# Long-run loads, one pool of accumulator banks, 2.25 frequency blocks and an inverse DFT by parity in a Nyströmformer and Hyena kernel

## The chip, the cores and the metric

The kernel runs on one core of a Trainium2 chip. The metric is device time in microseconds (us) of one execution; most executions of one kernel agree within 0.3 to 1%. A run is "slow" when it is over 1.5% above the fastest of the same kernel; ratios use fast runs alone. Besides the time, each run has one profiled execution, whose span (first to last instruction) is a few us shorter than the time.

Engines: PE is TensorE (matrix products), DVE is VectorE, ACT is ScalarE, POOL is GpSimd, which also issues the loads. Products write to an accumulator memory (PSUM), whose eight banks this kernel shares out among its buffer pools; an eviction is a DVE or ACT copy out of it.

## The reference, cut to what matters

```python
# q, k, v: [8 batches, 8 heads, 576 rows, 64]; m = 32 landmarks, scale = 1/8
q_lm = q.reshape(B, H, m, 18, D).mean(axis=3);  k_lm likewise
A  = softmax(scale * q    @ k_lm^T)          # 576 x 32 per head
Bm = softmax(scale * q_lm @ k_lm^T)          # 32 x 32
C  = softmax(scale * q_lm @ k^T)             # 32 x 576
Z  = Bm^T / (norm1 * norminf + 1e-6);  6 times: Z = 2 Z - Z Bm Z     # Newton
x  = (A @ Z @ C @ v)                         # heads side by side: [8, 576, 512]
x1, x2, x3 = split(x @ w_proj)               # 3 x 512 columns
x2c = irfft(rfft(x2, over rows) * rfft(filter, over rows))
out = (x1 * x2c * x3) @ w_out                # [8, 576, 512]
```

The kernel calls the first part of a batch its attention and the second its gate. It keeps the factors `ZC` (Z C v) and `A` apart, so that the projection works on `G = ZC @ w_proj` and the forward DFT on A. A real DFT of 576 rows has 289 frequencies; they are split by parity, so that only 288 rows are transformed.

## The kernel before

The parts that the change and the argument touch (cuts marked with `# ...`):

```python
ps_w: 2 buffers of 2 banks (big products)      # 4 banks
ps_t: 2 buffers of 1 bank, ps_s: 2 of 1 bank   # 2 + 2 banks

def load(b):                                   # k and q in runs of 64 floats = 256 bytes
    for c in range(NC): nc.gpsimd.dma_start(kn[:, c], kv[c])      # 6 transfers
    for c in range(NC): nc.gpsimd.dma_start(qn[:, c], qv[c // 3, c % 3])
    # ... v in 2 transfers, runs of 1,536 bytes

def attention(b):
    # ... landmark sums of head pairs (ps_s); 48 transposes into ps_t; Bm, its scaled inverse start (ps_s)
    for cc in range(3):
        RZ = newton(RZ, False)                 # ps_s, evicted by ACT and DVE
        pc = ps_t.tile(...)                    # scores of C, ps_t
        # ... 8 products, then exp on ACT
    # ... the same for A; C v into a ps_w buffer
    nc.vector.tensor_reduce(rA, eA, ...)       # row sums of A's softmax
    # ... A, AE (even and odd rows), AT (transposed A)

def gate(b, ZC, AE, AT):
    # ... G parts 1, 0, 2 and the forward DFT of A
    for f in range(3):                         # 3 frequency blocks of 96 rows
        # ... 4 products of 512 columns; X = copy (ACT); T = X * HH; Y = T0 + T1 (DVE)
    for j in range(4):
        # ... x1 (ACT) and gt = x1 * x3 (DVE), 8 products
        pi = wtile()                           # inverse DFT over 576 columns
        for f in range(3):
            for t in range(2):
                for e in range(2): matmul(pi[:, e, 0:288], Y[:, f, t, 128 j...], INV[:, f, t, 288 e...])
        nc.vector.tensor_tensor(y[:, j], pi, gt, op=mult)
    # ... out = y @ w_out in 5 row blocks (ps_t), copy, store

att = {0: attention(0)}; tables_fwd(); tables_inv(); filter_spectrum()
for b in range(8):
    load(b + 2); att[b + 1] = attention(b + 1); gate(b, *att.pop(b))
```

The order on each engine is made by a scheduler when the program is built; it mixes attention b+1 with gate b. Each engine then runs its own queue in that order.

The softmax here doesn't subtract the row's maximum and nothing guards it: scores larger than these inputs give would overflow.

## Time and profile before

The three runs before had a median of 358.37 us.

| what | value | view |
|---|---|---|
| span | 352.5 us | page |
| gate 0 starts / ends | 64.7 / 94.3 us | timeline, first G product and last output product |
| from the end of a gate to the end of the next | 38.0 us | timeline |
| PE busy in such an interval | 33.2 us | windows |
| gate 7 and the last stores | 323.5 to 352.5 us | timeline |

"Interval" below always means the third row: from the end of one gate's last output product to that of the next. The page of the kernel before; the first lines give busy us with the share of the span, the rows of digits the busy tenths in 40 slices, `q0` the queue of the loads:

```profile
span 352.5 us, 6549 instructions
...
PE 285.1 (81%) x2640; PEld 184.3 (52%) x2640; DVE 217.5 (62%) x464; ACT 159.5 (45%) x263; POOL 94.3 (27%) x150
...
PE   0586867699889899879888888979987988698793
...
PEclk9999999999999999999999999999999999999999
...
q0 software_dynamic: 82928, 16.85, 56.1%
```

The windows of two intervals (start and end, length; busy us with the number of instructions by engine; granted PE clock; DMA share; GB/s). The second has no load issues on POOL, and is as long:

```profile
209.29:247.33 38.04, 33.22 (x330) 21.53 (x330) 24.70 (x51) 18.40 (x31) 10.48 (x14) 1.00 0.72 79
...
247.00:285.00 38.00, 33.18 (x329) 21.53 (x327) 24.45 (x51) 18.38 (x31) 0.00 (x0) 1.00 0.11 32
```

PE is busy for 87% of an interval and far ahead of DVE and ACT. The timeline of PE: start, length, line, tiles, count, and the idle time before it with its cause. At the head of an interval, transposes (`pt`) and Newton pairs (`s<-RZ`) take turns, with waits on single evictions; later come waits of about a us on G and gt:

```profile
209.22 0.43 PE L161 MATMUL pt<-ident,kn 96*128 96x96 bf16 x6
209.49 0.30 PE L220 MATMUL s<-RZ 128*128 128x160 f16 x2
210.20 0.42 PE L161 MATMUL pt<-ident,kn 96*128 96x96 bf16 x6 [0.41 <-DVE kT L166]
...
220.38 0.90 PE L446 MATMUL w<-F,AE 96*128 96x288 f16 x6 [1.10 <-ACT G L439]
...
229.60 0.65 PE L476 MATMUL w<-AT,G 128*128 128x288 f16 x4 [0.78 <-ACT X L461]
...
232.66 0.65 PE L476 MATMUL w<-AT,G 128*128 128x288 f16 x4 [1.14 <-DVE gt L483]
```

The records of products overlap (a product of the inverse has a record of 287 ns, and the next one starts 132 ns after it). Charging each product only the time until the next one starts, or its own end where it comes earlier, a Newton product costs 130 ns in the kernel before (12 in an interval, 1.56 us).

### The profile page before, as it was taken

The numbers are of one execution on the slowest core, as the hardware profiler recorded it, in microseconds if no ns is written. First come the engines' busy times: TensorE is split into PE (matmuls) and PEld (weight loads), VectorE is DVE, ScalarE is ACT, GpSimd is POOL, SyncE is SP. The second block draws the span as 40 slices with busy tenths as digits, with TensorE's granted clock in tenths as the row PEclk, the third lists the DMA queues.
The fourth block names the chain that finished last, engine by engine and source line by source line (L and its number), as shares of the span: only waits on it lengthen the run. The fifth ranks groups of instructions, "written<-read, shape, count | busy, mean of one in ns | idle before, by whom it ended". The sixth has DMA issues, their size and how long they took to land.

```text
span 352.5 us, 6549 instructions
## 1 busy us (share of the span) xinstructions
PE 285.1 (81%) x2640; PEld 184.3 (52%) x2640; DVE 217.5 (62%) x464; ACT 159.5 (45%) x263; POOL 94.3 (27%) x150
## 2 busy tenths in 40 slices
PE   0586867699889899879888888979987988698793
PEld 0374743366465557546564646645754655364361
DVE  0148698987547854796456754785468656751651
ACT  1042263764366226542466237622654156625512
POOL 9934967700091006500280009200000000000000
PEclk9999999999999999999999999999999999999999
DMA  5999999930499019900694049901300050004104
GB/s 35 132 205 171 169 101 123 124 58 0 111 124 105 2 46 145 138 10 0 145 127 68 2 116 112 111 0 39 100 0 2 0 137 0 2 0 113 25 0 134
DMA packets 88718, 26.70 MB, mean 76 GB/s; under 512 B 76720, under 2 KB 83376, under 8 KB 88688
## 3 DMA queue, kind: packets, MB, share of 16 engines
q0 software_dynamic: 82928, 16.85, 56.1%
q1 hardware_dynamic: 5760, 9.44, 9.8%
q8 instruction: 20, 0.33, 0.4%
q14 instruction: 10, 0.08, 0.1%
HBM read 33.69 MB, written 9.44 MB: 122 GB/s over the span
## 4 chain that ended last, share of the span: by engine, by line
PE 50%; DVE 24%; ACT 10%; DMA 7%; POOL 4%; issue 3%; SPq 0%; DVEq 0%; ACTq 0%; POOLq 0%
PE w L488 9%; PE po L500 8%; DVE T L463 8%; PE w L476 6%; PE pt L161 4%; PE w L434 4%; DMA kn<-in_k_dram 4%; DVE y L492 4%; PE w L446 4%; PE w L265 3%; DVE gt L483 3%; ACT G L439 3%; ACT X L461 2%; PE pa L254 2%; PE pc L238 2%
## 5 line engine op out<-in xcount | busy, mean ns | idle before, releaser
L111 POOL DMA_DIRECT2D kn<-in_k_dram x48 | 37.2, 787 | 113.1 <-PE pt L161 111.7
L488 PE MATMUL w<-INV,Y 96*128 96x288 f16 x384 | 54.8, 287 | 0.2
L476 PE MATMUL w<-AT,G 128*128 128x288 f16 x256 | 41.7, 284 | 15.8 <-DVE gt L483 8.7
L500 PE MATMUL po<-wout,y 128*128 128x512 bf16 (+1 forms) x160 | 42.1, 380 | 5.3 <-ACT os L506 3.2
L463 DVE TENSOR_TENSOR T<-X,HH 96x2048 bf16<-96x2048 bf16 x24 | 28.7, 1217 | 24.0 <-ACT X L461 24.0
L488 PEld LDWEIGHTS <-Y 96*128 96x128 bf16 x384 | 35.1, 98 | 14.7 <-DVE Y L465 5.9
L476 PEld LDWEIGHTS <-G 128*128 128x128 bf16 x256 | 24.6, 96 | 32.5 <-issue 25.2
L113 POOL DMA_DIRECT2D qn<-in_q_dram x48 | 37.2, 783 | 9.7 <-DMA wproj<-in_moe_w_proj_dram 7.1
L506 ACT COPY os<-po 128x512 f32<-128x512 f32 (+1 forms) x32 | 18.7, 584 | 33.0 <-PE po L500 32.3
L492 DVE TENSOR_TENSOR y<-w,gt 128x576 bf16<-128x576 f32 x32 | 24.2, 757 | 15.0 <-PE w L488 15.0
L439 ACT CAST G<-w 128x1024 bf16<-128x1024 f32 x24 | 23.5, 1014 | 14.4 <-PE w L434 14.4
L166 DVE COPY kT<-pt 128x576 bf16<-128x576 bf16 x24 | 10.9, 457 | 26.2 <-PE pt L161 25.7
L500 PEld LDWEIGHTS <-y 128*128 128x128 bf16 (+1 forms) x160 | 14.7, 100 | 22.2 <-issue 8.6
L461 ACT CAST X<-w 96x1024 bf16<-96x1024 f32 x24 | 23.5, 1008 | 4.5 <-DVE T L463 3.2
L457 PE MATMUL w<-G,Ah 128*96 128x512 bf16 x96 | 23.8, 377 | 2.1 <-ACT G L439 1.4
L294 DVE TENSOR_REDUCE rA<-eA 96x48 f32<-96x1536 bf16 x8 | 14.0, 1748 | 15.0 <-ACT eA L258 15.0
L225 ACT CAST RZ<-s 128x256 f16<-128x256 f32 x40 | 14.9, 372 | 15.8 <-PE s L220 11.0
L446 PE MATMUL w<-F,AE 96*128 96x288 f16 x96 | 14.5, 285 | 8.4 <-ACT G L439 7.7
L226 DVE TENSOR_TENSOR RZ<-RZ,s 128x64 f16<-128x64 f16 x48 | 10.5, 218 | 14.5 <-ACT RZ L225 10.6
L434 PE MATMUL w<-wproj,ZC 128*64 128x512 bf16 x96 | 18.2, 390 | 0.5 <-ACT Ah L449 0.5
L220 PE MATMUL s<-RZ 128*128 128x160 f16 (+1 forms) x96 | 14.6, 235 | 4.9 <-DVE RZ L226 2.4
L161 PE MATMUL pt<-ident,kn 96*128 96x96 bf16 x192 | 15.3, 221 | 3.5 <-DVE kT L166 2.6
(205 smaller groups left out, 480.3 us busy)
## 6 DMA issues: line engine op xcount, KB each, us to landing
kn<-in_k_dram POOLq DMA_DIRECT2D x48, 96.0 KB, 4.3
qn<-in_q_dram POOLq DMA_DIRECT2D x48, 96.0 KB, 4.1
out_dram<-os SPq DMA_DIRECT2D x24, 192.0 KB, 2.5
out_dram<-os SPq DMA_DIRECT2D x24, 128.0 KB, 2.3
vb_103<-in_v_dram POOLq DMA_DIRECT2D x8, 288.0 KB, 6.3
vb_105<-in_v_dram POOLq DMA_DIRECT2D x8, 288.0 KB, 6.7
wproj<-in_moe_w_proj_dram POOLq DMA_DIRECT2D x1, 1536.0 KB, 13.7
out_dram<-os SPq DMA_DIRECT2D x24, 64.0 KB, 2.0
```

The lines of the kernel that those rows point to most:

```text
L111: nc.gpsimd.dma_start(kn[:, c], kv[c])
L113: nc.gpsimd.dma_start(qn[:, c], qv[c // 3, c % 3])
L161: nc.tensor.matmul(pt[:, c * R:(c + 1) * R], src[:, c, 2 * x:2 * x + 2, :].rearrange("p h d -> p (h d)"), ident[:R, :R], is_transpose=True ...
L434: nc.tensor.matmul(pg[64 * pp:64 * pp + 64, g, :], ZC[:, 2 * g + pp, :, :].rearrange("p h l -> p (h l)"), wproj[:, 2 * g + pp, Dm * jb:Dm ...
L439: nc.scalar.copy(G[:, :, Dm * jb:Dm * (jb + 1)], pg)
L446: nc.tensor.matmul(pf[:, par, 0:HS], AE[:, par, c, 128 * g:128 * g + 128], F[:, c, :, lo:lo + Q], start=(c == 0), stop=(c == 2))
L461: nc.scalar.copy(X, px[:R])
L463: nc.vector.tensor_tensor(T, X.unsqueeze(2).to_broadcast([R, 2, 2, Dm]), HH[:, f], op=ALU.mult)
L476: nc.tensor.matmul(px[:, e, 0:HS], G[:, g, lo:lo + P], AT[:, g, HS * e:HS * e + HS], start=(g == 0), stop=(g == 1))
L488: nc.tensor.matmul(pi[:, e, 0:HS], Y[:, f, t, P * j:P * j + P], INV[:, f, t, HS * e:HS * e + HS], start=(f == 0 and t == 0), stop=(f == NF ...
L492: nc.vector.tensor_tensor(y[:, j, :].rearrange("p (e s) -> p e s", e=2), pi[:, :, 0:HS], gt, op=ALU.mult)
L500: nc.tensor.matmul(po[:n], y[:, j, i0:i0 + n], wout[:, j, :], start=(j == 0), stop=(j == 3))
```

## The change

Its intent: fewer, longer loads; fewer PE columns in the gate; fewer evictions in front of Newton. The diff, cut to its core:

```diff
-    ps_t = ... bufs=2      # one bank each
-    ps_s = ... bufs=2
+    ps_a = ... bufs=4      # one pool of four for all single-bank tiles, C v included
@@ loads
-        for c in range(NC): nc.gpsimd.dma_start(kn[:, c], kv[c])            # 256-byte runs
+        nc.gpsimd.dma_start(kn..., k[b].rearrange("h (p c) d -> p h (c d)", c=NC))   # 1,536
+        for e in range(2): nc.gpsimd.dma_start(qn[:, :, 3e:3e+3, :]..., ...)         # 768
+    load_k(0); load_q(0)                         # ahead of the constants
@@ attention: row pairs of one head, folded by a second product
+        # pk, pq: 24 + 24 small products; Pk, Pq: copies on ACT
+        mm(pj[:, 0:256], Jf, Pk, ...)            # and four of 128 columns for q
+        nc.vector.tensor_copy(lm[0:64, :, :, 0, :], pj4[0:64])
+        nc.scalar.copy(lm[64:128, :, :, 1, :], pj4[64:128])
-        # 8 evictions of 576 columns after the transposes
+        # 6 evictions of 768 columns
@@ inverse tables
-        # t, u, sine, sign: about 9 us of DVE
+        mm(pt, F[:, c, par, 128 t...], identh, is_transpose=True)     # transposes of F
@@ gate: 2.25 blocks, then the two other G parts
-        for f in range(3): ...                   # 96 rows each
+        for par in range(2): ...                 # 128 rows each
+        # the last 33 frequencies: 16 products of 32 x 256 in quarters of one bank
+        g_part(0); g_part(2)                     # were ahead of the spectrum
@@ inverse by parity: E and O over 288 columns, 24 products and not 48
-        nc.vector.tensor_tensor(y[:, j], pi, gt, op=mult)
+        nc.scalar.copy(EO[:, par], pi)           # 4 evictions a gate
+        sd = EO[:, 0] + EO[:, 1]  and  EO[:, 0] - EO[:, 1]            # DVE
+        nc.vector.tensor_tensor(y[:, 2jp:2jp+2], sd, gt, op=mult)
@@ output: the last 64 rows in two column halves, side by side in one bank
```

## The prediction

> **What bounds the kernel now.** Timeline: gate 0 starts at 65 us; gates 0 to 6 end every 38.0 us (chain of waits: last output products at 91.5, 129.5, 206.4, 244.5, 282.5); gate 7 alone takes 323.5 to 352.5.
> - Steady state: the window 208.5 to 246.5 has TensorE busy 33.2 of 38.0 us, VectorE 24.7, ScalarE 18.4, clock 1.00. TensorE is the bound, with 5 us of short waits on evictions. Loads are not: the window 247 to 285, without load issues, also takes 38.0.
> - Prologue: 256-byte loads of k and q. Last q lands at 18.3 us, k of batch 1 at 35.6 (a 14.2 us DMA piece of the chain); POOL waits for DMA between 21 and 32, so the table iotas run only at 37.6; VectorE's tables hold the chain from 45 to 55.5, then the filter products (12 in 4.9 us).
>
> **Removed and added, per batch** (rates: back-to-back products in the timeline).
> - Inverse DFT: 48 products of 288 columns become 24; 12 took 1.49 us, so -3.0 us of TensorE.
> - Spectrum: 12 products of 512 columns become 8, plus 16 of 256 into quarter columns; 0.24 us each; the gate's two-way split products ran 8 in 1.05 us, so I estimate four together: -0.5. Output: the last row block splits in two: -0.4.
> - Landmark fold and smaller products: +0.5. TensorE net: -3.3 us.
> - VectorE: one of three T and Y pairs goes (-1.22 -0.68), transposed copies 6 instead of 8 (-0.4), tail +0.5, y even, output copy +0.3: -1.2 us.
> - ScalarE: E and O evictions (4 of 0.64, +2.6), landmark copies and fold (+1.2), one X for a small one (-0.4), one output copy less: +3 us, to 21.5.
>
> **What lies on the critical path.** The freed TensorE time is on it, but the two double-bank buffers now turn over faster than their evictions: a 288-column pair fills in 0.5 us and is evicted in 0.64 to 0.76 plus a wait, so I expect 1 of the 3.3 us back as waits. The path from the last inverse product to the output product grows by about 1.6 us (eviction, sum, difference, product), mostly covered by the next attention; shorter spectrum work gives about 1 back. Period 38.0 -> about 35.1 us: -20 over seven gates. Gate 7, uncovered: -2.
>
> Prologue: v, in 1536-byte runs, landed 2.9 us after q; k in that shape should take 3 us, not 7.7, and is issued before the constants. q lands near 10, k of batch 1 before 28. Inverse tables (VectorE 9 us) become transposes. Gate 0 should begin near 52: -13 us.
>
> The Trainium skill ("DMA: Bandwidth & Descriptors", section "Why small descriptors are slow (HBM only)") says each descriptor carries a fixed cost; the trace agrees in direction (38 ns per mostly 256-byte packet, queue table).
>
> **Prediction.** Span 352.5 -> 318, time 358.4 -> **324 us**, 80% range 307 to 343. Chances: faster by over 2% 0.94, within 2% 0.04, slower 0.02.
>
> **What would show it.** Software queue packets fall from 82,928 to about 25,000; inverse products count 192, TensorE busy about 255 us; the interval of output products 34 to 36.5 us; gate 0 begins at 48 to 56 us; ScalarE about 180 us busy.
>
> **What would make it wrong.** Quarter-column products that don't run together (+1 us a batch); evictions on ScalarE in front of the Newton copies, or the E/O, sum, product path, holding the period at 37 (time 338); a prologue still bound by tables and filter (+7). If the waits vanish too, 310.

## The result, and the profile after

The kernel after took 314.08 us (median of 4, 313.01 to 315.73), the kernel before 357.75. The ratio is 0.8797 with a 95% interval of 0.8756 to 0.8838. A ratio here is the mean time of one kernel's fast runs over that of the other's fast runs of the same rounds, so it isn't quite the ratio of the medians quoted. The output is correct, and the time lies in the predicted range (307 to 343), 10 us under the point of 324.

The page after, with the lines that answer to those above:

```profile
span 313.3 us, 6555 instructions
...
PE 254.5 (81%) x2684; PEld 162.1 (52%) x2684; DVE 201.2 (64%) x461; ACT 178.1 (57%) x301; POOL 40.3 (13%) x91
...
PE   0758279999798979987998799879989898978781
...
PEclk9999999999999999999999999998999799999997
...
q0 software_dynamic: 26480, 16.85, 39.0%
```

Two intervals of the kernel after. The second has a granted clock of 0.95:

```profile
154.24:186.39 32.15, 28.50 (x331) 18.35 (x332) 23.23 (x53) 20.94 (x36) 3.67 (x5) 1.00 0.57 93
186.39:220.15 33.76, 30.12 (x331) 18.86 (x331) 23.23 (x53) 20.94 (x36) 3.67 (x5) 0.95 0.54 89
```

Some forecasts held to a few per cent: packets of the load queue 26,480 (about 25,000), inverse products 192 (192), PE busy 254.5 us (255), ACT busy 178.1 us (180), gate 0 starts at 52.2 us (48 to 56). By the `q0` lines, a packet took 38 ns for 203 bytes before and 74 ns for 636 bytes after, so longer packets moved the same bytes in less DMA time. The distribution of the gain over the run did not hold:

| part of the span | before | after | gain | forecast |
|---|---|---|---|---|
| to the end of gate 0 | 94.3 us | 89.7 us | 4.7 | about 16 (13 + one gate's 2.9) |
| gates 1 to 6 | 229.2 us | 196.4 us | 32.7 | 17.4 (6 x 2.9) |
| gate 7, last stores | 29.0 us | 27.2 us | 1.8 | 2 |
| span | 352.5 us | 313.3 us | 39.2 | about 35 |

The interval is 32.15 us at full clock, not 35.1, and the prologue gained a third of what was forecast. The two errors had opposite signs, so that the sum came out near the forecast by luck. Per interval, PE's records answer as follows (us, charged as above; kernel before at 209.29, after at 122.1):

| PE work in an interval | before | after | measured | forecast |
|---|---|---|---|---|
| inverse DFT | 6.36 | 3.14 | -3.2 | -3.0 |
| spectrum | 2.69 | 2.95 | +0.3 | -0.5 |
| output product | 4.96 | 4.22 | -0.7 | -0.4 |
| Newton | 1.56 | 0.75 | -0.8 | none |
| all PE work | 33.2 | 28.5 | -4.7 | -3.3 |
| PE idle | 4.8 | 3.6 | -1.2 | +0.4 (1 as waits, less than 1 of it paid back) |

The quarter-column products do run side by side: 15 of them took 0.62 us, one alone 0.27. This agrees with the Trainium skill ("TensorEngine Tiling (Array Packing)", section "When to Use Tiling"), which gives four-way column tiling for a stationary operand of 32 columns.

A chain that the kernel before didn't have now stands in the gate. From the chain of waits of the kernel after (start, length, what):

```profile
171.03 0.60 ACT eA L273
...
171.66 1.75 DVE rA L312
...
173.89 0.69 DVE Cv L294 x2
...
175.41 0.87 DVE A L318
...
177.11 0.46 DVE AE L324
...
177.87 0.45 DVE AT L331
178.31 0.68 DVE y L523
...
179.03 1.04 PE po L540 x4
```

From 171.66 us on DVE works 6.6 us without a pause, nearly all of it for attention b+1 (row sums `rA`, then `Cv`, A, AE, AT), and the first half of `y` of gate b stands in its queue behind that. PE stands meanwhile for 1.5 us. And the timeline of PE shows that the same products take twice as long in the prologue:

```profile
56.86 2.13 PE L201 MATMUL pt<-ident,qn 96*128 96x96 bf16 x24
...
125.58 1.18 PE L201 MATMUL pt<-ident,qn 96*128 96x96 bf16 x24
...
146.89 1.04 PE L540 MATMUL po<-wout,y 128*128 128x512 bf16 x4 [1.53 <-DVE y L523]
```

The profile's own record of the clock begins at 64.3 us with full rate; before it, all products are at half rate (a 512-column product starts 0.43 us after the one before it there, 0.22 later). In the kernel before, full rate begins at 60.7 us. The Trainium skill ("TensorE: Matmul & The Clock Gate", section "What's actually happening") describes it: "the default state is throttled, and activity releases the throttle." The trace agrees with the two rates.

### The profile page after: what moved, and what is told of

Read it like the earlier page. It is cut to its first block, busy times and chain, and to the rows that moved or that the text cites. A ratio compares the mean times of both kernels' runs of the same rounds, so it can differ in the third digit from the quotient of the medians.

```text
span 313.3 us, 6555 instructions
## 1 busy us (share of the span) xinstructions
PE 254.5 (81%) x2684; PEld 162.1 (52%) x2684; DVE 201.2 (64%) x461; ACT 178.1 (57%) x301; POOL 40.3 (13%) x91
## 3 DMA queue, kind: packets, MB, share of 16 engines
q0 software_dynamic: 26480, 16.85, 39.0%
q1 hardware_dynamic: 6400, 9.44, 10.7%
## 4 chain that ended last, share of the span: by engine, by line
PE 35%; DVE 32%; ACT 15%; DMA 7%; issue 6%; POOL 3%; SPq 0%; ACTq 0%; DVEq 0%; POOLq 0%
PE po L540 7%; DMA filt<-in_moe_filter_fft_dram 5%; PE pt L201 5%; DVE rA L312 4%; PE w L515 4%; DVE y L523 3%; DVE gt L508 2%; PE w L451 2%; PE w L463 2%; PE w L501 2%; DVE T L468 2%; DVE A L318 2%; DVE sd L521 2%; ACT X L466 2%; PE pc L270 2%
## 5 line engine op out<-in xcount | busy, mean ns | idle before, releaser
L519 ACT CAST EO<-w 128x576 bf16<-128x576 f32 x32 | 20.5, 639 | 47.8 <-PE w L517 46.7
L540 PE MATMUL po<-wout,y 128*128 128x512 bf16 x128 | 33.2, 393 | 12.2 <-DVE y L523 11.6
L508 DVE TENSOR_TENSOR gt<-w,x 128x576 bf16<-128x576 f32 x32 | 23.5, 752 | 6.7 <-ACT x L506 5.6
L515 PE MATMUL w<-IV,Y 128*128 128x288 f16 x128 | 26.3, 299 | 0.2 <-DVE gt L508 0.2
L506 ACT CAST x<-w 128x576 bf16<-128x576 f32 x32 | 20.8, 650 | 7.4 <-PE w L501 6.6
L463 PE MATMUL w<-G,Ah 128*128 128x512 bf16 x64 | 18.9, 398 | 4.5 <-ACT Ah L453 4.5
L468 DVE TENSOR_TENSOR T<-X,HH 128x2048 bf16<-128x2048 bf16 x16 | 19.3, 1220 | 3.6 <-ACT X L466 3.6
L466 ACT CAST X<-w 128x1024 bf16<-128x1024 f32 x16 | 16.0, 1012 | 8.1 <-PE w L463 7.9
L451 PE MATMUL w<-F,AE 96*128 96x304 f16 x96 | 19.6, 314 | 0.0
L517 PE MATMUL w<-IV,Y 128*128 128x288 f16 x64 | 19.1, 298 | 0.0
L70 POOL DMA_DIRECT2D kn<-in_k_dram x8 | 6.4, 805 | 93.7 <-PE pt L201 88.5
L262 DVE TENSOR_TENSOR RZ<-RZ,pn 128x64 f16<-128x64 f16 x48 | 10.4, 216 | 12.1 <-ACT RZ L261 12.0
```

The costliest lines, as they stand in the source:

```text
L451: mm(pf[:, par, 0:TW], AE[:, par, c, 128 * g:128 * g + 128], F[:, c, par, :], start=(c == 0), stop=(c == 2))
L463: mm(px[:, t, :], Ah[:, g, par, 128 * t:128 * t + 128], G[:, g, Dm:2 * Dm], start=(g == 0), stop=(g == 1))
L466: nc.scalar.copy(X, px)
L468: nc.vector.tensor_tensor(T, X.unsqueeze(2).to_broadcast([P, 2, 2, Dm]), HH[:, par], op=ALU.mult)
L506: nc.scalar.copy(x1, px[:, :, 0:HS])
L508: nc.vector.tensor_tensor(gt[:, ji], px[:, :, 0:HS], x1, op=ALU.mult)
```

## The experiments

All times are medians of at least 4 runs, ratios against the kernel before, measured in the same rounds. The interval is that of the profiled execution, at full clock. All twelve experiments gave right results. tables_first and warm_start, in which two and three of four runs count as slow, are told in the text alone.

| kernel | time, us | ratio | interval | PE busy in it | gate 0 ends |
|---|---|---|---|---|---|
| before | 357.75 | 1 | 38.0 | 33.2 | 94.3 |
| before_one_pool | 339.89 | 0.9524 | 33.7 | 31.6 | 104.8 |
| new_attention_old_gate | 329.80 | 0.9254 | 34.3 | 32.4 | 91.7 |
| old_attention_new_gate | 367.80 | 1.0221 | 34.75 (one gate) | 29.2 | 101.8 |
| pools_apart | 324.11 | 0.9109 | 33.4 / 33.8 | 28.6 / 29.1 | 92.8 |
| short_loads | 322.36 | 0.9047 | 32.2 | 28.1 | 96.3 |
| old_order | 316.94 | 0.8887 | 31.9 | 27.9 | 89.4 |
| full_inverse | 314.97 | 0.8834 | 32.6 | 30.2 | 87.5 |
| after | 314.08 | 0.8797 | 32.15 | 28.5 | 89.7 |
| sum_in_parts | 304.67 | 0.8547 | 31.0 | 27.8 | 89.2 |
| warm_and_parts | 300.97 | 0.8435 | 31.0 | 27.8 | 86.8 |
| longer_warm_and_parts | 299.32 | 0.8383 | 31.0 | 27.8 | 82.1 |

### Undo one part of the kernel after

**The loads.** Six and six transfers of 256-byte runs into the new layout:

```diff
-        nc.gpsimd.dma_start(kn..., k[b].rearrange("h (p c) d -> p h (c d)", c=NC))
+        for c in range(NC): nc.gpsimd.dma_start(kn[:, :, c, :], kv[c])
```

> The kernel after, but k and q are again loaded as 6 + 6 transfers of 256-byte runs into the new layout; nothing else changes. Theory (loads matter in the prologue only): the interval from gate to gate stays at 32.1 us at full clock (within 0.3 us); the end of gate 0 moves later than 89.7 us, by 4 to 9 us, so the time is 318 to 323 us. Rival (the short loads, with their descriptor work on POOL, also slow the steady state): interval 33 us or more, time over 325 us.

Interval 32.2 us, gate 0 ends at 96.3 us, 6.6 later, time 322.36 us. The theory holds: the long runs are worth nothing in an interval and about 8 us by the medians. Of that the profiled runs show 6.6 us up to the end of gate 0, which include a stretch of 3.41 us at half rate in gate 0 (87.8 to 91.2 us) that the kernel after doesn't have there.

**The inverse.** Forty products over both halves of the rows (the tables get a signed second half), y straight from the accumulator:

```diff
-            EO = ...; sd = ...                   # 24 products, E and O on ACT, sum and difference
+            for par, t, e: mm(pi[:, e, 0:HS], Y[:, par, t, P*j:P*j+P], IV[:, par, t, e, :])
+            for e:         mm(pi[:, e, 0:HS], Y2[:, P*ji:P*ji+P], IV2[:, jp, e, :])
+            nc.vector.tensor_tensor(y[:, j], pi[:, :, 0:HS], gt[:, ji], op=ALU.mult)
```

> The kernel after, with the inverse DFT taken over all 576 columns again (40 products of 288 columns a gate, 24 before this edit), y = product times gt straight from the accumulator, no E and O evictions, no sum and difference. Theory (TensorE's own time bounds the gate, so 16 products of 125 ns are paid for in full): interval 32.1 -> 34.0 to 34.6 us, time 327 to 331 us. Rival (ScalarE's 2.6 us of E and O evictions and the longer path to y give most of the gain back): interval 32.1 to 33.0 us, time 314 to 320 us.

The rival holds. One interval of this kernel, in the windows view:

```profile
153.90:186.47 32.57, 30.21 (x344) 20.41 (x347) 23.11 (x51) 18.29 (x32) 3.66 (x5) 1.00 0.55 92
```

PE works 1.7 us longer than in the kernel after and ACT 2.65 us shorter, but the interval is only 0.4 us longer, and the prologue is 2.2 us shorter; the time, 314.97 us, can't be told from 314.08. Part of that tie is the clock: in the profiled run of full_inverse the full rate begins at 55.3 us and not at 64.3, and no gate from 1 to 6 has a half-rate stretch, where the kernel after has two (1.65 us each). At full clock the inverse is worth 0.4 us an interval: beside the rest of the change, the item that I had costed as the largest gain brings 0.4 of its 3 us. It moved the bound from PE towards the chain through DVE shown above: PE waits 0.3 us for `y` in this interval, and 1.5 us in the kernel after. Whether it would bring more with that chain shortened (sum_in_parts, below) was not run.

**The pools.** Two pools of two banks again, C v in a double bank:

```diff
-    ps_a ... bufs=4
+    ps_t ... bufs=2   # pt, pc, ptA, po        ps_s ... bufs=2   # pk, pq, pj, psB, psC, pn, pz
```

> The kernel after, with the four single banks of the accumulator split in two pools of two again, as before the change, and the C*v product in a double bank again. Theory A (the sharing of the four banks is what took about 1 to 1.5 us of waits and exposed result latency off each gate): interval 32.1 -> 33.3 to 34 us, time 322 to 328 us. Theory B (the order of work, not the banks, did it): interval within 0.4 us of 32.1, time 312 to 318 us.

The two intervals, in the windows view:

```profile
126.64:160.06 33.42, 28.64 (x322) 19.20 (x325) 22.93 (x50) 20.54 (x33) 3.66 (x5) 1.00 0.53 90
160.06:193.89 33.83, 29.12 (x333) 19.68 (x335) 23.89 (x56) 22.03 (x39) 3.66 (x5) 1.00 0.52 87
```

Interval 33.4 and 33.8 us in turn, time 324.11 us. Theory A holds, with 1.3 to 1.7 us a gate for the sharing and the place of C v together.

**The order of the G parts.**

```diff
         dft(1)
+        g_part(0); g_part(2)
         # spectrum
-        g_part(0); g_part(2)
```

> The kernel after, with the two other G parts again ahead of the spectrum products, as before the change. Theory B (starting the spectrum products at once lets VectorE's T and Y run while TensorE makes the other G parts, which took 1 us or more off each gate): interval 32.1 -> 33 to 34 us, time 320 to 328 us. Theory A (the banks did it): interval within 0.4 us of 32.1, time 312 to 318 us.

Interval 31.9 us at full clock: no cost. The time is 316.94 us; the profiled run had four intervals of 33.3 to 34.5 us at a clock of 0.95, about which more below; that is two half-rate stretches more than in the kernel after, of 1.65 us each, enough for the difference in time. Theory B falls.

### Take one part alone

The first joins the loads, the attention and the pool of four of after with the tables, filter spectrum and gate of before; as a diff to the kernel after:

```diff
-    tables_fwd, tables_inv, filter_spectrum, gate   # of after: 2.25 blocks, parity
+    tables_fwd, tables_inv, filter_spectrum, gate   # of before: 3 blocks, 48 products
```

> Half of the change: loads, landmarks, transposes and the four shared banks as after; tables, spectrum, inverse DFT and output product as before. The full-column inverse alone turned out to cost 0.4 us a gate, so the question is where the 5.9 us of a gate went. Theory A (the attention half: its products and evictions now fill the waits of the gate): interval 33 to 35 us at full clock, time 325 to 338 us. Theory B (the gate half: 4 us less work on TensorE and 1.2 us less on VectorE): interval 36 to 38 us, time 340 to 355 us.

The second is the other half, again as a diff to the kernel after:

```diff
-    load_k, load_q, load_v, attention               # of after
+    load, attention                                 # of before
-    ps_a = ... bufs=4
+    ps_t = ... bufs=2;  ps_s = ... bufs=2           # the gate's tiles in ps_t
```

> The other half: loads, attention and the two pools of two banks as before; tables, 2.25 frequency blocks, inverse by parity and split output as after. Theory A (attention half carries it): interval 36 to 37.5 us, time 335 to 350 us. Theory B (gate half carries it): interval 33 to 35 us, time 320 to 333 us. If both halves come out near 34 to 35 us, the two gains overlap: either frees enough, and together they add less than their sum; if both come out over 36, they need each other.

The third is the kernel before with this edit, and `pv` taken from the same pool:

```diff
-    ps_t = ... bufs=2;  ps_s = ... bufs=2
+    ps_a = ... bufs=4
```

> The kernel before with one edit: its two pools of two single banks become one of four, and the C*v product is taken out of the double banks. Parting the banks cost the kernel after 1.3 to 1.7 us a gate. Theory (the sharing works by itself): interval 38.0 -> 36.3 to 37 us, time 342 to 350 us. Rival (it pays only with the shorter gate, where TensorE has idle time): interval over 37.5 us, time 352 to 359 us.

One interval of before_one_pool in the windows view:

```profile
138.46:172.13 33.67, 31.58 (x330) 20.79 (x331) 23.96 (x52) 17.98 (x31) 10.53 (x14) 1.00 0.81 89
```

And a piece of the same interval in its PE timeline, where Newton pairs (`s<-RZ`) are followed at once by other products:

```profile
147.28 0.30 PE L219 MATMUL s<-RZ 128*128 128x160 f16 x2
147.42 0.51 PE L237 MATMUL pc<-lmbd,kT 128*96 128x64 bf16 x8
147.76 0.61 PE L457 MATMUL w<-G,Ah 128*96 128x512 bf16 x2
148.30 0.30 PE L219 MATMUL s<-RZ 128*128 128x160 f16 x2
```

Sharing the four banks, C v among them, with not one product fewer, took 4.4 us off the interval of the kernel before: 33.7 us. PE idle fell from 4.8 to 2.1 us, and the Newton product from 130 to 61 ns, because the scheduler now puts scores (`pc`) and spectrum products behind each Newton pair. In the kernel before, where Newton and scores had two banks each, a good part of attention b+1 stood in a row at the head of the interval. I had not listed the pools among the changes at all. The Trainium skill ("Perfetto Trace Analysis", section "Optimization Strategy") says of consistent bubbles that there may not be enough SBUF or PSUM for the next tile to be allocated; sharing what there is can be enough. Both runs on the pools, pools_apart and this one, move C v together with the sharing, so what each of the two is worth isn't shown. The expected time (342 to 350 us) was beaten, at 339.89, though less than the interval says: in the profiled runs 27.1 us came off gates 1 to 6, and 10.4 us were given back up to the end of gate 0 and 3.9 us in gate 7 and the last stores. Part of that is bookkeeping (at the end of gate 0 the kernel before has already made the landmarks and Bm of batch 2, this one not), part is half rate, which its clock record shows from 85.8 to 96.0 us and from 317.9 to 324.7.

new_attention_old_gate came out at 34.3 us, as theory A had it. So with the old gate the new attention gains nothing beyond its pool (33.7 without it). What it brings, together with the long loads, is in the prologue: gate 0 ends at 91.7 us, not at 104.8.

old_attention_new_gate is the surprise. Two of its intervals:

```profile
183.17:223.90 40.73, 35.49 (x320) 23.23 (x321) 23.65 (x54) 20.34 (x34) 10.52 (x14) 0.79 0.68 74
223.90:258.65 34.75, 29.17 (x320) 19.43 (x321) 23.40 (x54) 19.97 (x34) 10.52 (x14) 1.00 0.79 86
```

At full clock the gate half alone takes the interval to 34.75 us, so by that one gate the gains overlap: 4.4 us from the pool alone, 3.3 from the gate half alone, 5.9 together. But five of its six intervals took 40.2 to 40.8 us, because PE's clock fell to half for 17.07 us in each. All four runs show a low mean clock (0.871 to 0.907), and the kernel is no faster than the one before (ratio 1.0221, from two fast runs; the verdict was "unclear"). That the clock falls because PE is now less busy is what the skill's page on the clock gate would suggest. The trace speaks against that alone: cut into steps of 3.41 us from the first rise of the clock, it shows PE busy for 73 to 79% of the step before each of the five falls, but 56 to 65% of the step with transposes, while steps in which other products kept PE busy for 55% were followed by full rate. (In the one gate without a fall, a step of 81%, 69% with transposes, kept the rate.) No run varies this alone in this kernel, so the cause stays open.

### Where the rest of the prologue and of the interval is

**The tables.** The call of the forward tables moved ahead of the first attention:

```diff
-    att = {0: attention(0)}
     tables_fwd()
+    att = {0: attention(0)}
```

> The kernel after with the forward tables written ahead of the first attention in the program. In the trace of after, VectorE makes the tables from 35.8 to 43 us, after the whole first attention, and TensorE waits for them until 40.5; VectorE is idle for most of the first 12 us, but the iotas that feed the tables are on POOL behind the loads and start at 16 us. Theory (the tables bound the prologue): gate 0 ends 4 to 8 us earlier than 89.7 us, time 306 to 310 us. Rival (the filter load, which lands at 26.3 us, and the first attention's own chain bound it): within 2 us of 314.

The theory was not tested: the scheduler left the order on every engine as it was in the kernel after, and DVE still makes the tables from 36.1 us. Gate 0 ended at 90.1 us, time 314.33 us (two of four runs count as slow). Its runs of 310.07 to 317.60 us show how far one and the same order of work spreads.

**The sum of A's softmax in three parts**, to shorten the DVE chain of the interval:

```diff
         for cc in range(3):
             RZ = newton(RZ, cc == 2); scores(cc, qT, 0, eA)
+            nc.vector.tensor_reduce(rA[:, 16*cc:16*cc+16], eA[:, 2*cc:2*cc+2]..., op=ALU.add)
-        nc.vector.tensor_reduce(rA, eA..., op=ALU.add)
```

> The kernel after with the row sums of the softmax of A taken in three parts, each after its own exponential, in place of one reduction of 1.75 us after the last. In a gate of the kernel after TensorE stands for 1.5 us until y of the first half is made, behind VectorE's row of sum, reciprocal, A, AE, AT; the 3.4 us stretches at half clock (2 of 6 gates, 1.65 us each) all begin 24.7 to 26 us into a gate, where that wait is. Theory (this chain, not TensorE's work, bounds the gate now): interval 32.15 -> 30.8 to 31.6 us, fewer half-rate stretches, time 305 to 311 us. Rival (the wait moves elsewhere, or ScalarE and TensorE bound it together): interval within 0.4 us of 32.15, time 312 to 317 us.

One interval in the windows view:

```profile
151.34:182.32 30.98, 27.83 (x330) 18.62 (x332) 23.29 (x55) 20.83 (x36) 3.67 (x5) 1.00 0.59 97
```

The interval is 31.0 us with the same DVE work (23.3 us), the 1.5 us wait for `y` is gone, and no gate of the profiled run has a half-rate stretch. The time is 304.67 us, 3% under the kernel after and just below the 305 to 311 us expected. The edit also changed the scheduler's order elsewhere, so the 1.2 us belong to the edit with its new order and not to the reduction by itself.

**The half-rate stretches.** In five kernels with the wait for `y` (after, short_loads, old_order, tables_first, warm_start) the clock records of the profiled runs show 12 stretches of 3.41 us at half rate within gates 1 to 6, each worth about 1.65 us. All begin 24.0 to 26.0 us into their interval, where the wait for `y` is; sum_in_parts has none. That fits a clock that falls when PE stands still, but only some gates have one. The traces show what goes with it. Every change of the clock lies on a grid of 3.413 us, counted from the first rise of its trace. Before each of the 12 stretches PE was busy (charged as above) for 34 to 49% of the last step of that grid; every step in gates 1 to 6 of these kernels in which it was busy for 50% or more was followed by full rate, and between 45 and 49% both came. An interval of 32.15 us is 9.4 steps, so the same wait falls now into one step, now across two. This is read from the traces; no run moved the wait on purpose.

**The rate of PE in the prologue.** Twelve products that nobody reads, in the 5 us in which PE waits for the tables:

```diff
     att = {0: attention(0)}
+    pw = atile("warm")
+    for i in range(12):                          # 22 in longer_warm_and_parts
+        mm(pw, att[0][2][:, 0, 0:P], att[0][2][:, 0, 0:512], start=True, stop=True)
     tables_fwd()
```

> The kernel after with 12 products added (128x128 by 512 columns, of the first attention's transposed A, into a bank that nobody reads; the result stays right). They stand in the TensorE queue between the first attention and the forward tables, where TensorE waits from 35.1 to 40.45 us; the rest of the order is the same. In the records TensorE's clock goes from half to full rate at 64.3 us, in the kernel before at 60.7 us, and a 512-column product takes 0.44 us before and 0.22 us after that point. Theory (from 40 to 64 us the prologue is TensorE work at half rate, because the activity before had not released the clock): the clock rises by 42 us, gate 0 ends 5 to 9 us before 89.7, time 305 to 309 us. Rival (evictions and VectorE bound that stretch, or these products don't release the clock): gate 0 ends within 2 us of 89.7, time 312 to 316 us.

> Both edits. If each theory holds, their gains add, as one lies in the prologue and the other in the gates: time 297 to 304 us. If only one holds, 304 to 311 us.

> The sum in parts, and 22 added products in place of 12. With 12, TensorE's clock rose to full at 39 to 41 us, TensorE then stood for 1.7 us waiting for the third part of the forward table, and the clock fell back to half at 44 to 46 us until 56 (warm_and_parts) or 65 us (warm_start). With 22 the added products last until the table is there. Theory (the clock stays released as long as TensorE has no such wait, and the stretch from 42 to 64 us is then bounded by TensorE's rate): full rate from about 41 us on without a break, gate 0 ends at 82 to 86 us, time 295 to 300 us. Rival (evictions, VectorE and the later start bound that stretch as well): gate 0 ends at 86 to 89 us, time 300 to 304 us.

With 12 products alone, the clock rose at 40.8 us and fell again at 44.2, after PE had stood for 1.6 us waiting for the last part of the forward table; full rate returned at 64.7 us, about where it was without them. The wait stands in brackets in PE's timeline:

```profile
43.58 0.34 PE L382 MATMUL pi<-identh,F 96*128 96x96 f16 x4 [1.61 <-ACT F L368]
```

Gate 0 ended at 89.7 us in the profiled run, as in the kernel after. The median was 315.09 us; three of the four runs count as slow, and the fast one took 309.02 us, so the time shows no gain and rules none out. So the clock did rise, and a wait of 1.6 us later went with its fall. With the sum in parts, full rate returned at 56.3 us and gate 0 ended at 86.8. With 22 products, which last until the table is there, the clock record shows full rate from 38.6 us to the end, and the same 24 transposes as above take 1.18 us in the prologue:

```profile
35.76 6.29 PE L565 MATMUL warm<-AT 128*128 128x512 f16 x22 [0.49 <-DVE AT L333]
...
51.89 1.18 PE L201 MATMUL pt<-ident,qn 96*128 96x96 bf16 x24
```

Gate 0 ends at 82.1 us, 7 us earlier than in sum_in_parts, so that stretch was bound by PE's rate. The median over six runs is 299.32 us (297.67 to 300.61), 5 us under sum_in_parts and under the kernel after by 15; against warm_and_parts (299.64 to 304.88) the difference of the medians is small, as when the clock rises varies from run to run.

## Why the prediction was right or wrong

The total was right: 314.08 us is in the range, and the change was faster by 12%, forecast 9.6%. That it came so near is partly luck, since the interval gained twice what was forecast and the prologue a third. Point by point:

1. **Loads bound only the prologue: right.** Intervals with and without load issues are equally long, and short_loads leaves the interval at 32.2 us.
2. **"TensorE is the bound, with 5 us of short waits on evictions": half right, and the half that mattered was under-weighted.** More than half of PE's idle time (4.8 to 2.1 us) and of the Newton products' latency (130 to 61 ns) went away once the single banks were shared and C v left the double banks. before_one_pool removes 4.4 of 38.0 us without removing work. This was the step that failed for the interval: "I expect 1 of the 3.3 us back as waits". The runs show 1.2 us of waits removed and 0.8 us of Newton latency removed, in place of waits added. The prediction read the new pool in the diff and gave it no term.
3. **"-3.0 us of TensorE" for the inverse: right as work (3.2 us), wrong as time.** Undone by itself it costs 0.4 us an interval and nothing in the total that can be told from noise (there the clock helped, see full_inverse). With the waits at the head of the interval filled, PE waited 1.5 us an interval for y, which stood in DVE's queue behind the row sum, A, AE and AT.
4. **Spectrum "-0.5": wrong sign (+0.3).** Four quarter products do run together, but the full-size products cost 268 ns each by the start of the next one, against 224 before, partly in waiting.
5. **"Gate 0 should begin near 52: -13 us": the start was right (52.2), the gain was not.** The step equated the start of gate 0 with the gain. In the kernel before, attention 1 was mostly made before gate 0; in the kernel after it starts at 48 us and runs inside gate 0, which takes 37.5 us and not 29.7. Also, q lands at 10.7 us and not at 18.2 (forecast: near 10), but the first Bm product comes 5.5 us after it and not 1.8, behind the fold and the transposes at half rate, so ZC of batch 0 is made at 34.2 us, only 1.0 us earlier than before.
6. **Not forecast: the half rate.** The stretch from 40 to 64 us is PE work at half rate. longer_warm_and_parts takes 7 us off it by keeping the rate up.
7. **Evictions and the longer path to y: partly as forecast.** The path is there (1.5 us wait for the first half of y), mainly because y stands behind attention's work in DVE's queue; the sum in parts removed it.

What stays open: what exactly lets the clock fall or rise; why old_attention_new_gate is hit in nearly every gate; and where the 1.1 us come from that are left between its one gate of 34.75 us and the 32.15 us of the kernel after, once the pool's 1.3 to 1.7 us are taken off. For the second there is a guess: its stretched intervals of 40.2 to 40.8 us are close to 12 grid steps (40.96 us), so that each gate meets the grid at nearly the same place. That is not tested.

## What to carry to other kernels

Before costing removed work on the engine that looks bound, ask what its queue waits for and which buffer pools keep independent work apart; here merging two small pools was worth more than halving a product. Cost a change as an interval between two equal points of the pipeline, and never as the time at which some stage starts, since other work can move across that point. Look for products that take twice their usual time: a few products nobody reads, placed where TensorE waits, can pay for themselves, as 22 did here; with 12, a wait followed before the real work and they did not keep the rate up.

## What the Trainium skill lacked or had wrong

- "TensorE: Matmul & The Clock Gate" gives about 3.4 us of sustained work as what releases the clock. In the kernel after, PE worked without a pause from 43.8 to 62 us (transposes, 96-row and 32-column products among it) and the clock rose only at 64.3 us; with 128x128 products of 512 columns it rose 2.8 us after the first of them (35.76 to 38.6 us). In the 3.4 us from 47.3 to 50.7 us all of these were products of 96 rows or with 32 stationary columns, and of such products the page doesn't say whether they count.
- Of transposes the same page says, in "Part 4: PE-mode transpose", that the full rate doesn't engage for them. Here it did: in old_order PE made nothing but transposes from 12.4 us on, and the clock rose at 15.9; in new_attention_old_gate it made nothing but transposes from 37.9 us on, and from 40.7 they started 42 ns apart in place of 80.
- The same page ties the fall to an idle window of about 3.4 us. Here the clock fell 0.6 us after a wait of 1.6 us (warm_start, 44.2 us), and stretches of 3.41 us at half rate came after grid steps in which PE was still busy for 34 to 49%. The length of the stretches and the grid of 3.413 us agree with the page's window.
- No page says that the record of the clock has no entry before its first rise: the page of the profile shows a clock of 9 tenths or more for the first 64 us, where 24 transposes take 2.13 us and not 1.18.
- "Perfetto Trace Analysis" names too few PSUM buffers as a cause of bubbles, but not that dividing the banks into pools can do it: one pool of four in place of two of two, with C v moved into it, took 4.4 us off 38.0.
